# Up projection of a gated feed-forward: the gate's and the value's matmuls issued in turn, each into its own PSUM bank

## The chip, the cores and the metric

The kernel runs on one core of a Trainium2 chip. Its engines work side by side, each through its own list of instructions: TensorE (PE in the profile, its weight loads PEld), VectorE (DVE), ScalarE (ACT), GpSimd (POOL), and SyncE (SP), which issues the DMAs here. They wait for each other by semaphores. The metric is the device time of one execution in microseconds; a run's time is compared with that of the kernel before on the same chip.

## The reference

A linear attention with decay runs over 768 tokens, for 4 sequences and 8 heads of 48 channels. Its output is the input of a gated feed-forward with 1536 hidden units:

```python
for t in range(S):
    kt, vt, rt = (k[:, :, t], v[:, :, t], r[:, :, t])
    cur = np.einsum('bhd,bhe->bhde', u[None] * kt, vt)
    y[:, :, t] = np.einsum('bhd,bhde->bhe', rt, state + cur)
    state = w[None, :, :, None] * state + np.einsum('bhd,bhe->bhde', kt, vt)
...
gate = 1.0 / (1.0 + np.exp(-(x @ w_gate)))
val = x @ w_val
return (gate * val @ w_out).astype(np.float32)
```

`x` is the attention's output as 3072 tokens of 384 channels; `w_gate` and `w_val` are 384 x 1536, `w_out` is 1536 x 384.

## The kernel before

**Tiles and blocks.** The 768 positions go in 12 chunks of 64, which makes 256 columns to a chunk with the four sequences. Two chunks are a tile of 512 columns, so there are six tiles. The 1536 hidden units go in 12 blocks of 128. A *burst* is the attention of one pair of heads of one chunk, 48 in all. A *block* of a tile is one up projection, its gating, and one down projection. The first tile's first four blocks run for each chunk alone, at half the width; this makes 76 blocks: 8 of 256 columns and 68 of 512.

**One block.** Operands are split in a high and a low part (`whi`, `wlo` of the weights, index 0 and 1 of the second axis of `x` and `h`), and a product is three matmuls: low by high, high by high, high by low (`PASS`). The up projection (`Moe.up`, its matmul is L333) sums over 3 x 128 channels, so the gate takes nine matmuls into one PSUM bank and the value nine into another. `Moe.gate` then runs a sigmoid of the gate's bank on ACT (L345), a product with the value's bank on DVE (L346), a copy that makes `h`'s high part on ACT (L347), and a subtraction that makes its low part on POOL (L348). `Moe.down` (L358) adds nine matmuls to three banks `acc` that stay open for the whole tile. Its order changes the output bank at each matmul; in a tile's last block the nine are sorted by output bank instead.

**Banks.** Five PSUM banks are shared under the name `ring` by the gate and the value of each block, by a burst's two score tiles (L245, L246, L255, L256) and by its result `y` (L283, L286). A bank can be written again when its last reader is done: for the gate that is the sigmoid, for the value the product on DVE.

**Order.** The program is a list of 81 steps; a step holds a burst, a block, or both. PE and SP keep the order in which the program issues their instructions (`manual_schedule`), while ACT, DVE and POOL are ordered by a planner that simulates the program when it is built. From step 9 on, a step issues on PE: the up projection of its block, the scores and outer products of its burst, the application of the burst before, and the down projection of the *previous* step's block. In earlier steps up comes behind the burst. Weights arrive as float64 words and are decoded on ACT, DVE and POOL (L175 to L191) in the steps of the first tile; attention is spread over the steps up to the second last tile, and the last tile's steps have none. `store` (L370 to L372) copies a finished tile's three banks and sends them off.

Of the kernel before, what the change touches and what calls it, by code (L numbers as in the profile page):

```python
# [10 lines left out]
F32 = mybir.dt.float32  # L11
# [8 lines left out]
DM, DF = H * D, 1536  # L20
P = 128
# [2 lines left out]
NP = H // 2  # L24
NF = DF // P
CT = B * C
# The program goes in steps of a burst of attention (a pair of heads of a chunk) and a block
# of the feed-forward. Bursts before the first block; blocks whose two chunks go separately;
# blocks of a later tile with a burst beside them; steps in which a burst goes first; the
# steps in which the weights of a block are loaded, and decoded.  # L30
PRE, HALF = NP + 1, 4
SPREAD = [1, 1, 1, 0, 1, 1, 1, 0, 1, 1, 0, 0]
EARLY = 9
LOADW = (-1, 1, 3, 4, 7, 9, 10, 11, 12, 13, 14, 15)
DECW = (1, 4, 5, 6, 9, 10, 11, 12, 13, 14, 15, 16)
# bursts that have more of their work on GpSimd, and on the vector engine
U_POOL, R_DVE = range(3), range(4)
TILES = [[c, c + 1] for c in range(0, NC, 2)]

# [2 lines left out]
def rwkv_then_moe(ctx: ExitStack, tc: tile.TileContext, wd, un, rk, vn, wt, out):  # L42
    nc = tc.nc
# [12 lines left out]
    xp = main.enter_context(tc.tile_pool(name="xp", bufs=2))  # L56
    xsp = main.enter_context(tc.tile_pool(name="xsp", bufs=1))

    # the tensor engine and the loads go in the order of the program
    order = ExitStack()  # L60
    order.enter_context(tc.manual_schedule(engines={mybir.EngineType.PE, mybir.EngineType.SP}))

# [1 line left out]
    wu = const.tile([P, 2, NP], F32, name="wu")  # L64
    nc.sync.dma_start(out=wu, in_=wd)
    w = wu[:, 0]

    # Of a pair of heads: by channel r | k, by token r | k.
    inp = {}
    vz = [const.tile([P, NP, 2, B, 64], F32, name=f"vz{i}") for i in range(2)]  # L70

# [29 lines left out]
    table = const.tile([P, 1], F32, name="table")  # L101
    nc.scalar.activation(table, ident[:, 0:1], AF.Sigmoid)

    # w^0 .. w^96, of each channel; a decay outside 1/2 .. 2, where the powers of a chunk
    # hold, raises the flag instead
    pw = const.tile([P, NP, 97], F32, name="pw")
    nc.vector.memset(pw[:, :, 0], 1.0)
    nc.vector.tensor_scalar(pw[:, :, 1], w, 0.5, 2.0, ALU.max, ALU.min)
# [9 lines left out]
    power(4, 4, 4)  # L118
    power(8, 8, 8)
    power(16, 16, 16)  # L120
    # w^(31 - j); the reverse is w^(i - 32)
    tabk = const.tile([P, NP, C], F32, name="tabk")
    nc.vector.tensor_copy(tabk[:, :, 0:32], pw[:, :, 31::-1])

# [4 lines left out]
    flag = const.tile([1, 1], I32, name="flag")  # L129

    def token_table():
        # w^(95 - j) with the tokens j on the partitions
        power(32, 32, 32)
        power(64, 32, 64)
        tnat_in = hp.tile([P, 512], F32, name="sg").rearrange("q (p a j) -> q p a j", p=NP, a=2)
        for p in range(NP):
            nc.vector.tensor_copy(
                tnat_in[:, p], pw[:, p, 95:31:-1].unsqueeze(1).broadcast_to([P, 2, C])
            )
        tps = ps.tile([P, NP, P], F32, name="ring")  # L140
        for p in range(NP):
            nc.tensor.transpose(
                out=tps[:, p], in_=tnat_in[:, p].rearrange("q a j -> q (a j)"), identity=ident
            )
        nc.scalar.copy(out=tabn[0:64], in_=tps[0:64, :, 64:112])
        nc.scalar.copy(out=tabn[64:128], in_=tps[64:128, :, 0:48])
# [9 lines left out]
        nc.vector.tensor_reduce(total, count[0:1, 0:NP], axis=mybir.AxisListType.X, op=ALU.add)  # L156
        nc.vector.tensor_scalar(flag, total, float(P * NP), None, ALU.is_lt)

# [1 line left out]
    # They come as the words of float64: the high one holds sign, exponent and 20 bits  # L160
    # of the mantissa. Read as float32 and scaled by 2^-112 its exponent is rebiased;
    # three places to the left it is float32's, and the low word's top bits follow.
    # Two slots to a block: first its words, a half to a slot, then the parts hi and lo.
    W3, WH = 3 * DM, 3 * DM // 2
    raw, w32, whi, wlo = {}, {}, {}, {}

# [23 lines left out]
            nc.scalar.copy(out=whi[f][:, c], in_=g)  # L190
            nc.gpsimd.tensor_tensor(wlo[f][:, c], g, whi[f][:, c], ALU.subtract)  # L191

# [1 line left out]
    xt, xs, T, q, sc, yp = {}, {}, {}, {}, {}, {}  # L194

    def bc_b(ap):
# [91 lines left out]
    def to_x(n):  # L288
        c, p = bursts[n]
        ti = next(i for i, cc in enumerate(TILES) if c in cc)  # L290
        if ti not in xt:
            xt[ti] = xp.tile([P, 3, 2, 512], F32R, name="xt")
            xs[ti] = xsp.tile([P, 2, 512], F32R, name="xs")
        x = xt[ti]
        co = CT * TILES[ti].index(c)
        cols = slice(co, co + CT)
        dst = xs[ti][:, :, cols] if p == 3 else x[:, p, :, cols]
        y = yp.pop(n)
        # the last pair of a chunk that is waited for leaves the rows of pair 3 alone
        alone = ti == 0 and p == ORDER[-1]  # L300
        for lo, hi in ((0, 48), (64, 112)) if alone else ((0, 112),):
            nc.scalar.copy(out=dst[lo:hi, 0], in_=y[lo:hi, 0:CT])
            nc.vector.tensor_tensor(dst[lo:hi, 1], y[lo:hi, 0:CT], dst[lo:hi, 0], ALU.subtract)

        def fill(j, cols):
            for lo, to in ((0, 48), (64, 112)):
                nc.sync.dma_start(
                    out=x[to : to + 16, j, :, cols].bitcast(F32),
                    in_=xs[ti][lo + 16 * j : lo + 16 * j + 16, :, cols].bitcast(F32),
                )  # L310

        if ti == 0 and not alone:
            fill(ORDER[-1] if p == 3 else p, cols)
        elif ti and p < 3 and c == TILES[ti][-1]:
            fill(p, slice(0, CT * len(TILES[ti])))

# [1 line left out]
    PASS = ((1, 0), (0, 0), (0, 1))  # L318

    class Moe:  # L320
# [2 lines left out]
            self.pair, self.h = {}, {}  # L323

        def up(self, f):
            self.pair[f] = []
            w = whi[f], wlo[f]
            for g in range(2):
                o = ps.tile([P, 512], F32, name="ring")
                k = 0  # L330
                for kt in range(3):
                    for a, b in PASS:
                        nc.tensor.matmul(  # L333
                            o[:, self.cols], w[a][:, g * DM + kt * P : g * DM + (kt + 1) * P],
                            self.x[:, kt, b, self.cols], start=(k == 0), stop=(k == 8),
                        )
                        k += 1
                self.pair[f].append(o)

        def gate(self, f):  # L340
            a, b = self.pair.pop(f)
# [6 lines left out]
            nc.gpsimd.tensor_tensor(h[:, 1, c], sg[:, c], h[:, 0, c], ALU.subtract)  # L348

        def down(self, f):  # L350
            # the banks' first write clears them whole, so the second half only adds
            h, w = self.h.pop(f), (whi[f], wlo[f])
            todo = [(k, d) for k in range(3) for d in range(3)]
            if f == NF - 1:
                todo.sort(key=lambda kd: kd[1])
            for k, d in todo:
                a, b = PASS[k]
                nc.tensor.matmul(  # L358
                    self.acc[d][:, self.cols], w[a][:, 2 * DM + d * P : 2 * DM + (d + 1) * P],
                    h[:, b, self.cols], start=(f == 0 and k == 0 and self.cols.start == 0),  # L360
                    stop=(f == NF - 1 and k == 2),
                )
# [10 lines left out]
                out=out[d * P : (d + 1) * P, dst], in_=o.rearrange("q (c t) -> q c t", t=CT)  # L373
            )

# [1 line left out]
    halves = [(0, g) for g in range(HALF)] + [(1, g) for g in range(HALF)] + [(2, g) for g in range(HALF, NF)]  # L377
    moe_items = [(0, h, f) for h, f in halves]
    for ti in range(1, len(TILES)):
        moe_items += [(ti, 2, f) for f in range(NF)]  # L380
    # bursts of tile t + 1 in the first steps of tile t
    nb0 = NP * len(TILES[0])
    plan = [(n, None) for n in range(PRE)]
    nxt = PRE
# [43 lines left out]
            store(accs[ti], slice(TILES[ti][0], TILES[ti][-1] + 1))  # L428

    for i, (n, it) in enumerate(plan):  # L430
        # loads, some steps ahead
        later = [k for k, _ in plan[i + 1 :] if k is not None]
        while later and nload < min(len(bursts), later[0] + 3):
            load(*bursts[nload])
            nload += 1
        for f in [f for f, at in enumerate(LOADW) if at == i]:
            load_weights(f)
        nn = n + 2 if n is not None and n + 2 < len(bursts) else None
        m = it and moe_of(it)
        early = i < EARLY  # L440
        if it and not early:
            m.up(it[2])
        if nn is not None:
            decayed(nn)
            decayed_by_token(nn)
        if it and not early:
            m.gate(it[2])
        if n is not None:
            scores(n)
            outer(n)  # L450
            post(n)
        if pend_b is not None:
            apply(pend_b)
            to_x(pend_b)
            c, p = bursts[pend_b]
            if p == ORDER[-1] and c + 2 < NC:
                load_v(c + 2)
            if pend_b == 0:
                load_v(1)
        pend_b = n  # L460
        if nn is not None:
            bonus(nn)
        for fj in [(f, j) for f, at in enumerate(DECW) if at == i for j in range(2)]:
            scale_words(*fj)
        if nn is not None:
            diag(nn)
        for fj in [(f, j) for f, at in enumerate(DECW) if at == i for j in range(2)]:
            join_words(*fj)
            if fj[1] == 1:
                split_weights(fj[0])  # L470
        if it and early:
            m.up(it[2])
            m.gate(it[2])
        if pend_m:
            finish(pend_m)
        pend_m = it
        if i == 24:
            range_flag()
    finish(pend_m)

# [1 line left out]
    order.close()  # L482
    main.close()
    bad = nc.values_load(flag[0:1, 0:1], min_val=0, max_val=1)
# [147 lines left out]
```

## Time and profile before

| What | Value |
|---|---|
| median of 3 runs | 620.98 us |
| lowest and highest run | 620.76 us, 622.1 us |
| profiled execution, first to last instruction (its span) | 618.9 us |
| median less span: what lies around it | 2.1 us |
| busy PE / PEld | 568.8 us / 460.1 us |
| busy DVE / ACT / POOL | 280.8 us / 242.5 us / 294.4 us |
| up projection's matmuls (L333) | 1368 |
| down projection's matmuls (L358) | 684 |

For the profiled execution the span is given, not a time of its own as for the runs, so the runs' median stands beside it. In the profile a row of the timeline has the start in microseconds from the span's beginning, the duration, the engine, the source line, the operation, the tiles written and read, the shape, and how many were merged ("x2"); in brackets is the engine's idle time ahead of it and what ended it. A matmul's duration is longer than the distance to the next matmul's start, since matmuls are pipelined and their ends are modelled: distances of starts are the measure of pace. The table of stretches gives, for a piece of time, the busy time of each engine, the number of its instructions, and the TensorE clock that was granted (1.00 is full).

### The profile page before, as it was taken

Reading aid. Unit: us, or ns where it says so; the run is one execution under the profiler, and the core shown is the slowest. Engines: PE = TensorE matmul, PEld = TensorE weight load, DVE = VectorE, ACT = ScalarE, POOL = GpSimd, SP = SyncE. Lnnn points to the kernel's source line nnn. Section 1 sums busy time; section 2 is a strip of 40 time slices with the busy share of each in tenths; the row PEclk is TensorE's granted clock in tenths of the full one; section 3 lists DMA queues with packets and bytes.
Section 4 is the critical chain, followed back from the end, with each engine's and each line's share of the span. In section 5 each row is a group of like instructions: output and inputs, shape, how many; then the busy total and the mean of one; then the engine's idle time right before and its main releaser. Section 6 shows DMA issues by size and latency. Waiting matters only on the chain. (4 is left out here: it accounts for less than half of the span.)

```text
span 618.9 us, 10939 instructions
## 1 busy us (share of the span) xinstructions
PE 568.8 (92%) x4298; PEld 460.1 (74%) x4298; DVE 280.8 (45%) x568; ACT 242.5 (39%) x656; POOL 294.4 (48%) x298
## 2 busy tenths in 40 slices
PE   1757789887999999999999999999999999999995
PEld 1657678665887877887887787878777777888883
DVE  8889989997043334253334144334253322101011
ACT  2737676654234334145334136334144311211111
POOL 7588999987345335245335237335333311212121
PEclk9868999999999999999999999999999999999998
DMA  7395677233031212331311331311331100010001
GB/s 235 124 295 162 199 252 241 86 115 72 1 112 31 68 41 64 72 111 31 81 43 49 73 112 31 94 39 40 72 112 30 31 10 10 22 38 1 0 1 56
DMA packets 21369, 50.42 MB, mean 81 GB/s; under 512 B 2656, under 2 KB 9312, under 8 KB 21312
## 3 DMA queue, kind: packets, MB, share of 16 engines
q1 hardware_dynamic: 21312, 49.66, 27.2%
q8 instruction: 36, 0.59, 0.4%
q14 instruction: 21, 0.17, 0.1%
HBM read 42.57 MB, written 4.72 MB: 76 GB/s over the span
## 5 line engine op out<-in xcount | busy, mean ns | idle before, releaser
L333 PE MATMUL ring<-xt,whi 128*128 128x512 f32 (+1 forms) x912 | 277.2, 387 | 0.0
L333 PEld LDWEIGHTS ring<-xt,whi 128*128 128x128 f32 x912 | 171.0, 192 | 36.6
L348 POOL TENSOR_TENSOR h<-sg,h 128x512 fp32r<-128x512 f32 (+1 forms) x76 | 98.4, 1294 | 201.8 <-ACT h L347 201.3
L333 PE MATMUL ring<-xt,wlo 128*128 128x512 f32 (+1 forms) x456 | 177.4, 389 | 7.2 <-POOL wlo L191 4.4
L346 DVE TENSOR_TENSOR sg<-ring,sg 128x512 f32<-128x512 f32 (+1 forms) x76 | 50.2, 661 | 216.2 <-PE ring L333 207.6
L234 ACT ACTIVATE T<-ident,q 64x64 f32<-64x64 f32 x384 | 102.1, 335 | 60.3 <-DVE q L229 58.8
L358 PE MATMUL acc<-h,whi 128*128 128x512 f32 (+1 forms) x456 | 115.3, 381 | 8.0 <-POOL h L348 7.6
L333 PEld LDWEIGHTS ring<-xt,wlo 128*128 128x128 f32 x456 | 87.4, 192 | 26.7 <-POOL wlo L191 4.9
L212 POOL TENSOR_TENSOR T<-inp,tabk 64x256 f32<-64x256 f32 x92 | 80.9, 879 | 53.0 <-DMA inp<-in_rk 30.1
L358 PEld LDWEIGHTS acc<-h,whi 128*128 128x128 f32 x456 | 83.0, 188 | 27.1 <-POOL h L348 9.4
L345 ACT ACTIVATE sg<-ring 128x512 f32<-128x512 f32 (+1 forms) x76 | 43.4, 571 | 128.6 <-PE ring L333 127.0
L347 ACT CAST h<-sg 128x512 fp32r<-128x512 f32 (+1 forms) x76 | 45.3, 596 | 109.6 <-DVE sg L346 109.5
L358 PE MATMUL acc<-h,wlo 128*128 128x512 f32 (+1 forms) x228 | 69.9, 406 | 0.2 <-ACT h L347 0.2
L215 POOL TENSOR_TENSOR inp<-inp 128x192 f32<-128x192 f32 x48 | 36.2, 756 | 49.9 <-DMA inp<-in_rk 48.3
L209 DVE TENSOR_TENSOR inp<-inp,tabk 128x256 f32<-128x256 f32 x48 | 27.9, 582 | 60.8 <-DMA inp<-in_rk 60.6
L262 DVE COPY_PREDICATED T<-causal,ring 64x256 f32<-64x256 int32 x96 | 43.0, 447 | 4.9 <-PE ring L256 2.2
L358 PEld LDWEIGHTS acc<-h,wlo 128*128 128x128 f32 x228 | 38.1, 188 | 9.4 <-ACT h L347 0.8
L191 POOL TENSOR_TENSOR wlo<-wf,whi 128x576 fp32r<-128x576 f32 x24 | 41.1, 1726 | 6.6 <-ACT T L234 5.0
L245 PEld LDWEIGHTS ring<-T,inp 48*64 48x64 f32 x384 | 28.0, 141 | 15.8 <-issue 12.2
L228 DVE TENSOR_TENSOR inp<-inp,uns 128x192 f32<-128x192 f32 x45 | 26.1, 580 | 28.9 <-POOL inp L215 28.9
L283 PE MATMUL ring<-T,vz 128*64 128x64 f32 x384 | 34.4, 236 | 3.2 <-ACT T L234 2.1
L246 PE MATMUL ring<-T,inp 48*64 48x64 f32 x384 | 34.3, 233 | 3.2 <-DVE vz L273 1.5
(54 smaller groups left out, 500.9 us busy)
## 6 DMA issues: line engine op xcount, KB each, us to landing
inp<-in_rk SPq DMA_DIRECT2D x48, 448.0 KB, 3.9
wr<-in_wt SPq DMA_DIRECT2D x24, 576.0 KB, 6.9
vz<-in_vn SPq DMA_DIRECT2D x24, 256.0 KB, 4.5
out_y<-o SPq DMA_DIRECT2D x18, 256.0 KB, 2.4
xt<-xs SPq DMA_DIRECT2D x30, 64.0 KB, 2.3
xt<-xs SPq DMA_DIRECT2D x12, 32.0 KB, 2.3
uns<-in_un SPq DMA_DIRECT2D x1, 96.0 KB, 5.4
wu<-in_wd SPq DMA_DIRECT2D x1, 4.0 KB, 1.6
```

The source lines that it names most:

```text
L191: nc.gpsimd.tensor_tensor(wlo[f][:, c], g, whi[f][:, c], ALU.subtract)
L212: eng.tensor_tensor(T[n][lo : lo + 64, k], t[lo : lo + 64, 0], bc_b(tabk[lo : lo + 64, p, ::-1]), ALU.mult)
L215: nc.gpsimd.tensor_tensor(u[:, 0], u[:, 0], u[:, 1], ALU.mult)
L234: nc.scalar.activation(T[n][lo : lo + 64, k, b], ident[lo : lo + 64, lo : lo + 64], AF.Copy, scale=q[n][lo : lo + 64, b : b + 1],)
L262: nc.vector.copy_predicated(T[n][lo : lo + 64, k], bc_b(cmask[lo : lo + 64, lo : lo + 64]), s[lo : lo + 64, 0:256].rearrange("q (b i) -> q ...
L283: nc.tensor.matmul(y[0:64, cs], z[:, 0, b], T[n][:, 0, b], start=True, stop=True)
L333: nc.tensor.matmul(o[:, self.cols], w[a][:, g * DM + kt * P : g * DM + (kt + 1) * P], self.x[:, kt, b, self.cols], start=(k == 0), stop=(k ...
L345: nc.scalar.activation(sg[:, c], a[:, c], AF.Sigmoid)
L346: nc.vector.tensor_tensor(sg[:, c], b[:, c], sg[:, c], ALU.mult)
L347: nc.scalar.copy(out=h[:, 0, c], in_=sg[:, c])
L348: nc.gpsimd.tensor_tensor(h[:, 1, c], sg[:, c], h[:, 0, c], ALU.subtract)
L358: nc.tensor.matmul(self.acc[d][:, self.cols], w[a][:, 2 * DM + d * P : 2 * DM + (d + 1) * P], h[:, b, self.cols], start=(f == 0 and k == 0 ...
```

## The change

The loop over the gate and the value goes inside the loop over the nine products: both banks are taken at the start, and the gate's product *k* is followed by the value's product *k*.

```diff
         def up(self, f):
-            self.pair[f] = []
             w = whi[f], wlo[f]
-            for g in range(2):
-                o = ps.tile([P, 512], F32, name="ring")
-                k = 0
-                for kt in range(3):
-                    for a, b in PASS:
-                        nc.tensor.matmul(
-                            o[:, self.cols], w[a][:, g * DM + kt * P : g * DM + (kt + 1) * P],
-                            self.x[:, kt, b, self.cols], start=(k == 0), stop=(k == 8),
-                        )
-                        k += 1
-                self.pair[f].append(o)
+            o = self.pair[f] = [ps.tile([P, 512], F32, name="ring") for _ in range(2)]
+            for k in range(9):
+                kt, (a, b) = k // 3, PASS[k % 3]
+                for g in range(2):
+                    nc.tensor.matmul(
+                        o[g][:, self.cols], w[a][:, g * DM + kt * P : g * DM + (kt + 1) * P],
+                        self.x[:, kt, b, self.cols], start=(k == 0), stop=(k == 8),
+                    )
```

Each product has the operands it had, and each bank gets its nine products in the same order. The weight that two neighbouring matmuls of one bank share (high by high and high by low) is no longer used twice in a row; the moving operand now is. The rest of the diff takes comments away.

## The prediction
> **What bounds the kernel now.** I read the page first, then the busy time by stretches, then the waits of PE, then the timeline at the places where the two banks of an up projection are filled and emptied. The page's head, its busy shares and its row of granted clock by fortieths:
>
> ```profile
> span 618.9 us, 10939 instructions
> PE 568.8 (92%) x4298; PEld 460.1 (74%) x4298; DVE 280.8 (45%) x568; ACT 242.5 (39%) x656; POOL 294.4 (48%) x298
> ...
> PEclk9868999999999999999999999999999999999998
> ```
>
> The shares are a mean over two very different stages, as the stretches show (length, then busy time of PE, PEld, DVE, ACT, POOL, then clock):
>
> ```profile
> 44.00:134.00 90.00, 74.98 (x804) 64.65 (x802) 85.88 (x150) 59.38 (x169) 84.71 (x75) 0.96 0.58 184
> 134.00:161.00 27.00, 23.32 (x94) 17.78 (x92) 16.66 (x23) 14.16 (x33) 19.13 (x14) 0.94 0.21 47
> 161.00:607.00 446.00, 446.00 (x3114) 357.18 (x3113) 138.82 (x313) 147.30 (x392) 159.41 (x169) 1.00 0.18 49
> ```
>
> From 44 to 134 us DVE is busy 85.88 of 90 and POOL 84.71: attention and the decoding of weights set the pace, and PE has holes. From 161 to 607 us PE is busy all the time at full clock. So in the first stage a delay of PE can vanish in a later hole; in the second every nanosecond of PE counts. The holes, from PE's waits (total, times, longest):
>
> ```profile
> PE acc L358 <- POOL h L348: 7.6, 5, 2.4
> PE ring L333 <- POOL wlo L191: 4.4, 3, 2.3
> PE ring L333 <- DVE sg L346: 2.9, 2, 2.7
> ```
>
> **The change, part by part.** No instruction is added or removed: 18 weight loads and 18 matmuls per block before and after, the same ACT, DVE and POOL work, the same DMAs. Three things move: the pace of the stream, the moment the gate's bank is full, and the moment the value's bank must be free.
>
> *Pace.* Two blocks of the steady end, starts of the matmuls (an entry "x3" is three in a row). First an up (565.47 is the gate's first, 567.57 the value's first), the down behind it and the next up; then the down of a tile's last block, which is sorted by output so that three matmuls in a row go to one bank:
>
> ```profile
> 565.47 0.40 PE L333 MATMUL ring<-xt,wlo 128*128 128x512 f32 x1
> ...
> 567.57 0.39 PE L333 MATMUL ring<-xt,wlo 128*128 128x512 f32 x1
> ...
> 569.66 0.86 PE L358 MATMUL acc<-h,wlo 128*128 128x512 f32 x3
> 570.36 1.52 PE L358 MATMUL acc<-h,whi 128*128 128x512 f32 x6
> 571.72 0.40 PE L333 MATMUL ring<-xt,wlo 128*128 128x512 f32 x1
> ```
> ```profile
> 539.13 0.39 PE L358 MATMUL acc<-h,wlo 128*128 128x512 f32 x1
> ...
> 540.49 0.40 PE L333 MATMUL ring<-xt,wlo 128*128 128x512 f32 x1
> ```
>
> The up takes 569.66 - 565.47 = 4.19 us, 232.8 ns a matmul; the last six of a down take 571.72 - 570.36 = 1.36 us, 226.7 ns. One could think that nine writes to one bank are slow and that the down is quick because it changes bank at every matmul. The sorted down speaks against it: its last six, in two runs of three to one bank and with the moving operand in the up's order, take 540.49 - 539.13 = 1.36 us too. And the up's halves take 2.10 and 2.09 us: the change of bank between them shows nothing. So I take the pace as unchanged, 0 us. The bound on the gain is the down's pace for all full-width up matmuls, whose counts are in the lines by form:
>
> ```profile
> L333 PE MATMUL ring<-xt,whi 128*128 128x512 f32 x816 | 257.3, 396 | 0.0
> L333 PE MATMUL ring<-xt,wlo 128*128 128x512 f32 x408 | 161.9, 397 | 2.9 <-DVE sg L346 2.9
> ```
>
> (816 + 408) x 6.1 ns = 7.5 us. On the other side I know no row of a slower alternation; the same 7.5 us is taken as its bound, by symmetry, an estimate.
>
> *The gate's bank is full later.* Its ninth matmul becomes the block's 17th, so the sigmoid no longer runs beside the value's matmuls. At the very end this is not hidden, because there only one down (2.06 us) stands between the last up and the down that needs its result:
>
> ```profile
> 604.58 0.63 PE L333 MATMUL ring<-xt,whi 128*128 128x512 f32 x2
> 605.31 0.60 ACT L345 ACTIVATE sg<-ring 128x512 f32<-128x512 f32 x1 [2.79 <-PE ring L333]
> ...
> 606.68 0.63 PE L333 MATMUL ring<-xt,whi 128*128 128x512 f32 x2
> 607.41 0.69 DVE L346 TENSOR_TENSOR sg<-ring,sg 128x512 f32<-128x512 f32 x1 [5.55 <-PE ring L333]
> 608.14 0.62 ACT L347 CAST h<-sg 128x512 fp32r<-128x512 f32 x1 [2.23 <-DVE sg L346]
> 608.84 1.28 POOL L348 TENSOR_TENSOR h<-sg,h 128x512 fp32r<-128x512 f32 x1 [4.95 <-ACT h L347]
> 610.17 0.50 PE L358 MATMUL acc<-h,whi 128*128 128x512 f32 x1 [0.36 <-POOLq L485]
> ```
>
> The sigmoid starts 0.10 us after the end of the gate's last matmul (605.21), the multiply 0.10 us after that of the value's (607.31). With the gate's last one matmul ahead of the value's, it ends at 607.31 - 0.23 = 607.08; sigmoid 607.18 to 607.78; a hop of 0.04 (608.10 to 608.14 in the row of the cast); multiply at 607.82 instead of 607.41. PE waits there already (to 610.17, for POOL's part at 610.12), so the whole shift lands on the end: **+0.41 us**. In the other blocks of the PE-bound stage another up of 4.19 us stands between, and the chain from 607.41 to 610.12 takes 2.7 us: it stays hidden, with over 3 us to spare.
>
> *The value's bank must be free earlier,* at the second matmul instead of the tenth: 8 x 0.2328 = 1.86 us. Where the tenth waited already, the wait starts sooner and ends at the same moment, and 17 matmuls follow it instead of 9. The rows: two blocks of the first tile, with the multiply that frees the bank of the second, and one place in the PE-bound stage where the sigmoid that frees a bank runs late:
>
> ```profile
> 106.88 0.64 PE L333 MATMUL ring<-xt,whi 128*128 128x512 f32 x2
> ...
> 109.05 0.50 PE L333 MATMUL ring<-xt,wlo 128*128 128x512 f32 x1 [0.16 <-DVE sg L346]
> ```
> ```profile
> 126.07 0.62 PE L333 MATMUL ring<-xt,whi 128*128 128x512 f32 x2
> ...
> 130.82 0.50 PE L333 MATMUL ring<-xt,wlo 128*128 128x512 f32 x1 [2.73 <-DVE sg L346]
> ```
> ```profile
> 130.09 0.68 DVE L346 TENSOR_TENSOR sg<-ring,sg 128x512 f32<-128x512 f32 x1
> ```
> ```profile
> 359.37 0.57 ACT L345 ACTIVATE sg<-ring 128x512 f32<-128x512 f32 x1
> ...
> 359.43 0.62 PE L333 MATMUL ring<-xt,whi 128*128 128x512 f32 x2
> ```
>
> At 359.43 the value's first matmul would stand; all other banks hold unread tiles, and the sigmoid ends at 359.94; with the hop of 0.05 (130.77 to 130.82) PE waits 359.99 - 359.43 = **+0.56 us**, uncovered. Everywhere else after 161 us a bank is free in time or nearly.
>
> In the first stage the two blocks end 1.86 us later each. The first falls into DVE's backlog. For the second, these are the waits that follow, the sigmoids of that block and the next, and the stretches of 3.41 us on which the granted clock changes:
>
> ```profile
> 143.65 0.50 PE L358 MATMUL acc<-h,whi 128*128 128x512 f32 x1 [1.08 <-POOL h L348]
> ```
> ```profile
> 152.56 0.97 PE L358 MATMUL acc<-h,whi 128*128 128x512 f32 x3 [2.37 <-POOL h L348]
> ```
> ```profile
> 137.62 0.58 ACT L345 ACTIVATE sg<-ring 128x512 f32<-128x512 f32 x1
> ```
> ```profile
> 142.41 0.59 ACT L345 ACTIVATE sg<-ring 128x512 f32<-128x512 f32 x1
> ```
> ```profile
> 126.39:129.80 3.41, 1.70 (x8) 1.04 (x6) 3.38 (x4) 1.59 (x3) 3.33 (x3) 1.00 0.58 223
> ...
> 150.28:153.69 3.41, 1.13 (x5) 0.95 (x6) 2.34 (x3) 1.50 (x5) 3.33 (x4) 1.00 0.00 0
> 153.69:157.11 3.42, 3.42 (x10) 2.65 (x9) 0.01 (x1) 2.08 (x8) 3.42 (x4) 0.50 0.00 0
> ```
>
> After a stretch with PE busy 1.13 of 3.41 us the clock is halved for the next one, costing about 3.42 / 2 = 1.7 us; after one with 1.70 it is not. With the change PE stands from about 126.5 to 130.82, so the stretch from 126.39 is nearly empty, and the matmuls from 130.82 to 133.21 run at half clock: 1.2 us more, a shift of 1.86 + 1.2 = 3.06 us. The waits that follow hold 1.08 + 2.37 = 3.45 us, and what ends them is ACT's and POOL's backlog: the sigmoid at 137.62 runs 4.4 us after its block's matmuls, so it is not made late. All is swallowed by 152.56, and the stretch before 153.69 is now filled, so the half clock there goes: between 0 and -1.7 us. The middle, **-0.85 us**, since the grid of stretches is not tied to the program. Two waits for POOL's wlo in half-width blocks start five matmuls sooner; they lie before 75 us, ahead of the same holes, and I take nothing.
>
> The Trainium skill, in "TensorE: Matmul & The Clock Gate", Part 1, has the same gate: a free-running window of about 3.4 us, half clock after an idle one. The trace agrees with the period (150.28, 153.69, 157.11), and shows it for a window that was a third busy, too.
>
> **Sum**, against the profiled execution: 0 + 0.41 + 0.56 - 0.85 = +0.12 us, span 619.0. The median of the runs, 620.98, is 2.1 us above that span, as what lies around it; so **621.1 us**.
>
> **The rivals.**
> 1. *The alternation is quicker.* Up goes at the down's 226.7 ns: -7.5 us, 620.98 + 0.97 - 7.5 = 614.5. For it: the two paces. Against: the sorted down and the seamless change of bank within the up. A part of it would give 617 to 619. Chance 0.12.
> 2. *The half clock goes for nothing and no bank is late,* because the planner, which orders ACT, DVE and POOL anew, frees banks sooner: 620.98 + 0.41 - 1.7 = 619.7. Chance 0.08.
> 3. *The swallowing fails* (slower). The next block's up begins here:
>
> ```profile
> 136.34 0.39 PE L333 MATMUL ring<-xt,wlo 128*128 128x512 f32 x1
> ```
>
> The place is the wait that ends at 152.56. Its releaser hangs on the sigmoid at 142.41, whose block starts at 136.34 and would end, shifted by 3.06 us, at about 143.6: later than ACT takes it now. If this, or a new order on ACT or POOL, moves POOL's part for that block by more than its slack of about 2 us, the delay stays in front of the PE-bound stage: 620.98 + 0.97 + 1.86 = 623.8, with the half clock 625.0; I take 624.4. For it: the sigmoid that becomes ready so late. Against: ACT and POOL are behind anyway. Chance 0.33.
> 4. *Cycling through banks throttles PE.* If PE paused between alternate banks so that the clock halved, the 1224 matmuls x 0.2328 = 285 us could take up to twice that, 285 us more. The down already changes bank at each matmul, at a clock of 1.00 from 161 to 607 us, so chance 0.02. The Trainium skill names this in the same page, "A second HAM failure mode: psum-queue depth-cycling"; the trace does not agree for the down.
>
> That the order isn't what the diff says is excluded: PE keeps the program's order.
>
> **How the numbers follow.** The forecast has 0.45, the rivals 0.12, 0.08, 0.33 and 0.02. About 0.2% (1.2 us) is what a measurement of this kernel can tell from no change. Rivals 1 and 2 are faster: 0.2; the forecast is within: 0.45; 3 and 4 are slower: 0.35. The range runs from a pace gained by half, 617, to rival 3 with half clock, 625.2; the full pace gain and the throttling are left out, some 0.15 with their fringes.
>
> **What would show it.** Starts of up matmuls 4.19 us apart per block (pace); sigmoid 0.1 us after the 17th matmul, multiply at once behind; PE's wait for POOL in the last down 0.4 us longer; a wait at the second matmul of an up near 359 us, of 0.56; a wait of over 4 us near 126; PE's start on the stage from 153 us no later than before. A pace off by 1 ns is worth 1.2 us and would make the prediction wrong; so would a new order on ACT, DVE or POOL that keeps PE waiting before 161 us.

## The result: slower by 1.5%

| | median | runs | ratio to before |
|---|---|---|---|
| before | 620.87 us (619.7 to 622.1) | 4 | 1 |
| after | 630.52 us (628.9 to 631.85) | 4 | 1.0154 [1.0131, 1.0178] |

The page of the changed kernel's profile, its head and its row of granted clock:

```profile
span 626.7 us, 10963 instructions
PE 577.9 (92%) x4298; PEld 468.0 (75%) x4298; DVE 280.9 (45%) x568; ACT 242.8 (39%) x656; POOL 295.6 (47%) x298
...
PEclk9997898889999999999999999999999999999998
```

Here the up's matmul is L331, the sigmoid L341, the product on DVE L342, the cast L343, the subtraction on POOL L344, the down L354. The span is 7.8 us longer; this execution is the fastest of its four runs, so the median lies further up. The table of stretches, with the columns as in the prediction:

```profile
44.00:134.00 90.00, 72.84 (x707) 64.07 (x707) 82.58 (x143) 58.70 (x167) 80.77 (x69) 0.85 0.50 163
134.00:161.00 27.00, 26.19 (x163) 20.27 (x162) 19.12 (x25) 11.67 (x25) 19.53 (x17) 1.00 0.37 108
161.00:619.00 458.00, 456.41 (x3155) 364.43 (x3154) 141.54 (x319) 151.60 (x405) 164.01 (x173) 1.00 0.17 48
```

The stage from 161 us is almost as full as it was (456.41 of 458 us; before, 446.00 of 446), at clock 1.00. Most of the loss is in the first stage: in the same 90 us PE has issued 707 matmuls instead of 804, DVE has done 143 instructions instead of 150 and POOL 69 instead of 75. The second tile's first up shows how much is lost by its start, in the timelines of before and after:

```profile
167.42 0.40 PE L333 MATMUL ring<-xt,wlo 128*128 128x512 f32 x1
```
```profile
173.39 0.62 PE L331 MATMUL ring<-xt,wlo 128*128 128x512 f32 x2
```

5.97 of the 7.8 us are there already. The waits of PE in the changed kernel:

```profile
PE ring L331 <- DVE sg L342: 7.3, 4, 3.7
PE ring L331 <- POOL wlo L191: 4.3, 3, 2.3
PE ring L331 <- DVE vz L273: 3.5, 2, 2.5
PE acc L354 <- POOL h L344: 1.9, 2, 1.0
```

The wait for POOL's `h` shrank from 7.6 to 1.9 us, and an up now waits for DVE instead: for the product (7.3 against 2.9), and for the attention's update of `vz`, which frees a score bank. But the sum of PE's waits didn't grow. The stretch from 44 us to the second tile's first up, before and after:

```profile
44.00:167.42 123.42, 104.72 (x921) 87.64 (x920) 103.23 (x173) 74.76 (x204) 105.30 (x90) 0.96 0.47 145
```
```profile
44.00:173.39 129.39, 111.42 (x920) 94.08 (x920) 104.39 (x172) 75.43 (x204) 104.10 (x88) 0.89 0.43 136
```

The work in it is the same to within two instructions of each engine. PE stands for 17.97 us instead of 18.70, and is busy for 6.70 us more, at a mean clock of 0.89 instead of 0.96. DVE stands for 25.0 us instead of 20.2, and POOL for 25.3 instead of 18.1. So the stretch is longer because of the slower clock, or because the other engines stand more; the section on the halved clock parts the two.

One place where an up waits for DVE, in PE's and in DVE's timeline:

```profile
107.09 0.39 PE L331 MATMUL ring<-xt,wlo 128*128 128x512 f32 x1
109.99 0.74 PE L331 MATMUL ring<-xt,wlo 128*128 128x512 f32 x1 [2.51 <-DVE vz L273]
```
```profile
105.60 1.56 DVE L228 TENSOR_TENSOR inp<-inp,uns 128x192 f32<-128x192 f32 x1 [0.49 <-POOL inp L215]
107.09 1.96 DVE L183 SCALAR_TENSOR_TENSOR wf<-wr,wf 128x576 int32<-128x576 int32 x1
...
109.43 0.41 DVE L273 SCALAR_TENSOR_TENSOR vz<-vz,pw,ring 48x192 f32<-48x192 f32 x1
...
110.54 0.34 DVE L229 TENSOR_REDUCE q<-inp 128x4 f32<-128x192 f32 x1
110.80 0.41 DVE L342 TENSOR_TENSOR sg<-ring,sg 128x256 f32<-128x256 f32 x1
```

The gate's first matmul runs at 107.09, the value's first 2.9 us later, when the update of `vz` at 109.43 is done. Meanwhile DVE works through decoding (L183) and the attention's L262 to L229, and the product of the block before comes behind them all. At this place PE waits for the attention, not for the product. In the kernel before that product runs ahead of all this:

```profile
97.22 1.03 DVE L209 TENSOR_TENSOR inp<-inp,tabk 128x256 f32<-128x256 f32 x1
98.17 0.41 DVE L346 TENSOR_TENSOR sg<-ring,sg 128x256 f32<-128x256 f32 x1
```

So DVE's list of instructions is no longer the same. PE keeps the program's order, but the planner orders ACT, DVE and POOL from its own simulation of the program, and the change moved that. The number of DVE's other instructions ahead of the product of the first tile's blocks 2 to 13, from the two programs:

```
block     2    3    4    5    6    7    8    9   10   11   12   13
before  102  117  130  136  151  159  168  182  197  211  223  231
after   105  118  133  138  153  163  180  189  204  216  231  233
```

The product stands later in every one, in the 8th block by twelve instructions (the place above). In all, 144 of DVE's 568 places hold another instruction than before, 148 of ACT's and 108 of POOL's. Two theories follow. **A:** the new order of ACT, DVE and POOL costs the time. **B:** PE's own order does, by the early bank or the late gate.

### The profile page after: what moved, and what is told of

Its sections match the earlier page's. It is cut to its first block, busy times and chain, and to the rows that moved or that the text cites. A ratio compares the mean times of both kernels' runs of the same rounds, so it can differ in the third digit from the quotient of the medians.

```text
span 626.7 us, 10963 instructions
## 1 busy us (share of the span) xinstructions
PE 577.9 (92%) x4298; PEld 468.0 (75%) x4298; DVE 280.9 (45%) x568; ACT 242.8 (39%) x656; POOL 295.6 (47%) x298
## 5 line engine op out<-in xcount | busy, mean ns | idle before, releaser
L331 PE MATMUL ring<-xt,whi 128*128 128x512 f32 (+1 forms) x912 | 245.8, 393 | 0.0
L331 PEld LDWEIGHTS ring<-xt,whi 128*128 128x128 f32 x912 | 172.9, 197 | 36.9
L344 POOL TENSOR_TENSOR h<-sg,h 128x512 fp32r<-128x512 f32 (+1 forms) x76 | 101.3, 1332 | 183.6 <-ACT h L343 182.0
L331 PE MATMUL ring<-xt,wlo 128*128 128x512 f32 (+1 forms) x456 | 145.0, 396 | 15.2 <-DVE sg L342 7.3
L342 DVE TENSOR_TENSOR sg<-ring,sg 128x512 f32<-128x512 f32 (+1 forms) x76 | 50.2, 661 | 204.8 <-ACT sg L341 199.1
L341 ACT ACTIVATE sg<-ring 128x512 f32<-128x512 f32 (+1 forms) x76 | 43.5, 573 | 230.5 <-PE ring L331 230.5
L212 POOL TENSOR_TENSOR T<-inp,tabk 64x256 f32<-64x256 f32 x92 | 79.5, 864 | 81.3 <-PE ring L286 45.0
L354 PE MATMUL acc<-h,whi 128*128 128x512 f32 (+1 forms) x456 | 115.0, 383 | 2.6 <-POOL h L344 1.9
L331 PEld LDWEIGHTS ring<-xt,wlo 128*128 128x128 f32 x456 | 87.7, 196 | 36.4 <-DVE sg L342 9.1
L354 PEld LDWEIGHTS acc<-h,whi 128*128 128x128 f32 x456 | 83.8, 191 | 20.7 <-POOL h L344 2.7
L354 PE MATMUL acc<-h,wlo 128*128 128x512 f32 (+1 forms) x228 | 70.8, 410 | 0.4 <-ACT h L343 0.4
L343 ACT CAST h<-sg 128x512 fp32r<-128x512 f32 (+1 forms) x76 | 45.3, 596 | 59.6 <-DVE sg L342 59.5
L209 DVE TENSOR_TENSOR inp<-inp,tabk 128x256 f32<-128x256 f32 x48 | 26.3, 547 | 89.2 <-DMA inp<-in_rk 89.1
L354 PEld LDWEIGHTS acc<-h,wlo 128*128 128x128 f32 x228 | 38.8, 191 | 10.0 <-ACT h L343 1.5
L262 DVE COPY_PREDICATED T<-causal,ring 64x256 f32<-64x256 int32 x96 | 43.0, 447 | 3.5 <-PE ring L256 0.5
```

The lines of the kernel that those rows point to most:

```text
L212: eng.tensor_tensor(T[n][lo : lo + 64, k], t[lo : lo + 64, 0], bc_b(tabk[lo : lo + 64, p, ::-1]), ALU.mult)
L262: nc.vector.copy_predicated(T[n][lo : lo + 64, k], bc_b(cmask[lo : lo + 64, lo : lo + 64]), s[lo : lo + 64, 0:256].rearrange("q (b i) -> q ...
L331: nc.tensor.matmul(o[g][:, self.cols], w[a][:, g * DM + kt * P : g * DM + (kt + 1) * P], self.x[:, kt, b, self.cols], start=(k == 0), stop ...
L341: nc.scalar.activation(sg[:, c], a[:, c], AF.Sigmoid)
L342: nc.vector.tensor_tensor(sg[:, c], b[:, c], sg[:, c], ALU.mult)
L343: nc.scalar.copy(out=h[:, 0, c], in_=sg[:, c])
```

## Experiments

Unless said otherwise a kernel is compared over three rounds with the kernel before on the same chip. An order is held by edges without a semaphore, put at the end of the program: they only tell the planner which instruction of an engine comes behind which. In the traces of the first two runs below the three engines run exactly the order that was to be held. Line numbers in these kernels differ; the tiles tell which instruction a row is. The diffs are shortened to what matters, with loops and conditions written in short.

### One half of the change at a time

```diff
     finish(pend_m)
+    for engine, places in ISSUE.items():
+        mine = [k for k in nc.cur_bb.bb.instructions if k.engine == engine and type(k).__name__ in COMPUTE]
+        for a, b in zip(places, places[1:]):
+            tc.add_manual_dep(mine[b], mine[a].name, NoSync, reason="issue order")
```

**The change on PE, the order of before elsewhere:**

> The change on PE as it is, but ACT, DVE and POOL issue their instructions in exactly the order that they had before the change (their order is pinned). Theory A (the planner's new order of ACT, DVE and POOL costs the time): about 621 to 622 us, the prediction's own sum, with +0.4 at the end and +0.6 near 359 us. Theory B (PE's order itself costs it: the value's bank is wanted sooner, the gate's is full later): about 630 us as with the change, whatever the order on the other engines.

Measured: 621.28 us, 1.0006 [0.9991, 1.0022].

**Nine and nine on PE, the changed kernel's order elsewhere:**

> The mirror image: PE issues nine gate matmuls and then nine value matmuls as before, but ACT, DVE and POOL are pinned to the order that they have with the change. Theory A: about 629 to 630 us. Theory B: about 621 us. If both share the cost, x1 and x2 lie in between and their excesses over before add up to about 9.7 us, or to less where they meet in the same holes.

Measured: 626.77 us, 1.0106 [1.0074, 1.0138].

Theory A holds in the main: PE's order alone costs nothing that can be measured. The other engines' order alone costs 1.1%, less than the 629 to 630 us that the theory asked for, and both together cost 1.5%. The two intervals just overlap (up to 1.0138, from 1.0131), so a part of the loss may need both.

Two more kernels take one part of PE's new order each, with before's order elsewhere:

```diff
-            for g, k in [(g, k) for g in range(2) for k in range(9)]:
+            for g, k in [(0, 0), (1, 0)] + [(0, k) for k in range(1, 9)] + [(1, k) for k in range(1, 9)]:   # early bank
+            for g, k in [(0, k) for k in range(8)] + [(1, k) for k in range(8)] + [(0, 8), (1, 8)]:         # late gate
```

**Early bank:**

> One part alone, with the other engines pinned to their order before: gate 0, value 0, then the gate's other eight and the value's other eight. The value's bank is wanted at the second matmul as with the change, but the gate's is full at the 10th matmul instead of the 17th. Theory B with the bank as its cause: as far above before as x1. Theory B with the late gate as its cause, or theory A: within 1 us of before (here I expect +0.6 near 359 us, nothing at the end).

Measured: 620.21 us, 0.9984 [0.9969, 0.9998]. Once more with five rounds:

> The kernel of the third run once more, with more rounds. If the early bank has a gain of its own: 0.9970 to 0.9995 again. If that was scatter: 0.9995 to 1.0015.

Measured: 620.16 us, 0.9993 [0.9975, 1.0010]. The value lies in the band for a gain of its own (0.9970 to 0.9995), but its interval takes in 1: a small gain is neither shown nor excluded.

**Late gate:**

> The other part alone, again with the other engines pinned to their order before: eight gate matmuls, eight value matmuls, then the last of each. The gate's bank is full at the 17th matmul, the value's bank is wanted at the 9th instead of the 10th. Theory B with the late gate as its cause: as far above before as x1. With the bank as its cause, or theory A: +0.4 us, the piece at the end of the kernel.

Measured: 621.86 us, 1.0017 [1.0002, 1.0032]. Its last up and the last down's wait:

```profile
604.99 0.40 PE L405 MATMUL ring<-xt,wlo 128*128 128x512 f32 x1
...
612.59 0.50 PE L428 MATMUL acc<-h,whi 128*128 128x512 f32 x1 [0.62 <-POOLq L569]
```

From one to the other it is 7.60 us. In the kernel before it is 7.22 (602.95, the first row of the fence below, to 610.17), and in the early-bank kernel 7.22 too. The late gate costs 0.38 us at the end, and the early bank nothing there.

### Which tile

```diff
+            turns = [(k, g) for k in range(9) for g in range(2)]
+            if self.ti == 0:            # in the mirror: self.ti > 0
+                turns.sort(key=lambda t: t[1])
+            for k, g in turns:
```

The planner is free in both. **In turn from the second tile on:**

> Nine and nine in the blocks of the first tile, in turn from the second tile on, planner free (its order in the first tile stays that of before). All of the loss in the first tile's order: 621.0 to 621.8 (the last block's 0.4 us and up to 0.6 us for a bank). Rival, a loss of pace or banks in the 60 later blocks: 624 or more.

Measured: 623.46 us, 1.0043 [1.0027, 1.0060], between the two theories. **In turn in the first tile alone:**

> In turn in the blocks of the first tile, nine and nine from the second tile on, planner free (it takes the new order of the changed kernel in the first tile). All of the loss in the first tile: 628.5 to 630.5. Rival, a loss in the later blocks: 624 to 626.

Measured: 626.67 us, 1.0101 [1.0077, 1.0125], less than expected. So about two thirds of the loss are made in the first tile, and there is a second one behind it, of 2.6 us where I had priced 0.41 and 0.56. In the changed kernel's trace 1.8 of the 7.8 us come behind the second tile's first up: 0.38 at the end, and most of the rest at one place, here on PE and on DVE:

```profile
373.58 0.40 PE L331 MATMUL ring<-xt,wlo 128*128 128x512 f32 x1
374.95 0.50 PE L331 MATMUL ring<-xt,wlo 128*128 128x512 f32 x1 [0.97 <-DVE sg L342]
```
```profile
373.87 0.42 DVE L209 TENSOR_TENSOR inp<-inp,tabk 128x256 f32<-128x256 f32 x1 [5.32 <-DMA inp<-in_rk]
374.21 0.69 DVE L342 TENSOR_TENSOR sg<-ring,sg 128x512 f32<-128x512 f32 x1
```

Here the product stands one place later, behind L209, and L209 waits for a load: DVE is idle for 5.32 us with the product behind it, and the up is 1.14 us late (374.95 - 373.58 = 1.37, less the pace of 0.23). In the kernel before, the same two instructions in the other order:

```profile
363.66 0.69 DVE L346 TENSOR_TENSOR sg<-ring,sg 128x512 f32<-128x512 f32 x1 [0.44 <-PE ring L333]
369.03 0.43 DVE L209 TENSOR_TENSOR inp<-inp,tabk 128x256 f32<-128x256 f32 x1 [4.68 <-DMA inp<-in_rk]
```

The load is late there too, and no product waits behind it. The run with turns from the second tile on has PE's wait at the same block (0.58 us, at 369.64).

### Which part of the new order

First with the planner free but for one edge per product on DVE:

```diff
+    for a, b in (each product of the first and later tiles, and its neighbour on DVE):
+        tc.add_manual_dep(mine[b], mine[a].name, NoSync, reason="issue order")
```

**Nine and nine, products held late:**

> Order as before on PE (nine and nine); every product on DVE is only held behind the DVE instruction that stands ahead of it in the changed kernel's program, and the planner orders all else as it likes. Theory, the late product on DVE alone (it keeps the value's bank and so PE): 625 to 628, near the 626.8 of the run with the whole new order. Rival, the rest of the new order (decoding and attention work on ACT and POOL): 621 to 622.

Measured: 629.69 us, 1.0153 [1.0129, 1.0177]: more than the whole new order gave under nine and nine. **The change, products held early:**

> The change on PE; every product on DVE is only held ahead of the DVE instruction that follows it in the program before, and the planner orders all else as it likes. Theory, the late product: 621 to 623, with no wait of PE at 107 us and about 4 us of it near 127. Rival, the rest of the new order: 628 to 630, as the changed kernel.

Measured: 622.38 us, 1.0027 [1.0005, 1.0048]: most of the loss is gone. Both times agree with the late product as the cause. PE's waits in the second run do not: there is no wait of 4 us near 127, and in all PE waits for the product as long as in the changed kernel (7.3 us):

```profile
PE ring L337 <- DVE sg L348: 7.4, 4, 2.9
```

Besides, the planner arranged the rest around the edges again (in the first of them, 118 places on DVE, 105 on ACT and 60 on POOL differ from before), so they don't isolate it. The next ones hold every place.

**One product later** (the change, before's order, the 8th block's product moved 8 places):

> The change on PE, the order of before on ACT, DVE and POOL, but for one instruction: DVE's product of the first tile's 8th block stands 8 places later (the changed kernel has it 12 later). If late products are the cause: a wait of PE of 2 to 4 us at the next up's second matmul (about 101 us), and 622.5 to 625 where the run without this had 621.3. Rival, one late product is swallowed like the two late uppings that were predicted: 621 to 621.8.

Measured: 621.7 us, 1.0015 [0.9992, 1.0037]. PE doesn't wait at the next up, but two and four blocks later:

```profile
110.53 0.50 PE L406 MATMUL ring<-xt,wlo 128*128 128x512 f32 x1 [1.85 <-DVE sg L417]
...
131.73 0.63 PE L406 MATMUL ring<-xt,wlo 128*128 128x512 f32 x1 [2.78 <-DVE sg L417]
```

They are no longer than without the move (5.7 us in two waits there, 4.6 here), and the time is the same: one late product is swallowed. **All products late,** nothing else moved, under nine and nine:

> Nine and nine, before's order on ACT, DVE and POOL, but DVE's products stand where the changed kernel has them (up to 8 places later; in three blocks 1 to 4 places short of it). Product's place is the cause: 624 to 627. Rival, the rest of the order: 620.5 to 621.5.

Measured: 628.34 us, 1.0109 [1.0089, 1.0129]. Under the change:

> The same order under the change on PE. Product's place: 627 to 630.5. Rival, the rest: 621 to 622.

Measured: 633.56 us, 1.0209 [1.0175, 1.0244]. Late products alone cost as much as the whole new order, or more; both times lie above the theory's range. **The mirror,** the changed kernel's order with the products alone put back:

> The change on PE with its own order on ACT, DVE and POOL, but DVE's products stand where before has them (in the 8th and the 10th to 13th block only part of the way). Product's place: 621 to 624. Rival, the rest: 628 to 630.5.

Measured: 630.67 us, 1.0159 [1.0135, 1.0182]. This is what the theory of the product's place forbids. Its DVE waits from 44 to 161 us say why:

```profile
DVE sg L417 <- ACT sg L416: 12.8, 9, 2.9
```

DVE takes the product up earlier and stands there for the sigmoid, which ACT still has late. So the next two move all four instructions of the gating (sigmoid, product, cast, subtraction). **Put back in the changed kernel's order:**

> The change on PE; decoding and attention in the changed kernel's order on ACT, DVE and POOL, but all four instructions of the gating where before has them (one product only part of the way). The gating carries the loss: 620.5 to 623.5. Rival, the new order of decoding and attention costs by itself: 627 to 631.

Measured: 636.15 us, 1.0237 [1.0199, 1.0275], the slowest of all, and above both ranges. **Put late in before's order:**

> The change on PE; decoding and attention in the order of before, all four instructions of the gating where the changed kernel has them (in three blocks 1 or 2 places short of it). The gating carries the loss: 628 to 632. Rival: 621 to 623.

Measured: 630.86 us, 1.0152 [1.0116, 1.0188].

| order under the change on PE | gating as before | gating late |
|---|---|---|
| decoding and attention as before | 1.0006 | 1.0152 |
| decoding and attention new | 1.0237 | 1.0154 (the change) |

So the place of one kind of instruction doesn't decide it. Late gating is enough for the whole loss where the rest stands as before. But with the new order of the rest, early gating is worse still, and then PE waits for the last of the gating, in one wait of its timeline for 6 us:

```profile
165.72 1.65 PE L429 MATMUL acc<-h,whi 128*128 128x512 f32 x3 [6.04 <-POOL h L419]
```

I read this as a matter of how the lists of three engines fit each other; what makes one set fit was not found. One count parts all these kernels, POOL's instructions from 44 to 134 us, here of the changed kernel with the early products and with the late gating:

```profile
44.00:134.00 90.00, 73.89 (x772) 63.48 (x771) 84.39 (x144) 58.58 (x168) 81.64 (x74) 0.92 0.56 181
```
```profile
44.00:134.00 90.00, 71.90 (x724) 63.28 (x723) 74.53 (x140) 55.92 (x162) 73.76 (x69) 0.87 0.53 170
```

Every kernel at 1.0057 or below has done 74 or 75 there, every kernel at 1.01 or above 68 to 71. DVE's count overlaps (143 to 150 against 138 to 146). The count marks how far the work has come; it is no cause.

### Products earlier than before

If late is bad, is earlier good? Five products of the first tile are put where their operands are there in the profile of before, first under nine and nine:

> Nine and nine as before, the order of before on all engines, but for five of DVE's products in the first tile (blocks 7, 9, 10, 11, 13), which stand 5, 2, 3, 4 and 1 places earlier, at the first place where their operands are there in the profile of before. If the product's place sets PE's waits: the 2.7 us wait near 131 us goes and the time is 617 to 619.5. Rival, what it is put ahead of (decoding, attention) is late instead: 620.5 to 622.

Measured: 622.91 us, 1.0031 [1.0011, 1.0051]. Under the change:

> The change on PE, the order of before, with the same five products earlier. If the product's place sets PE's waits: the 4.2 us wait near 128 us shrinks to under 2, and 617.5 to 620. Rival, as above: 621 to 622.5.

Measured: 624.26 us, 1.0057 [1.0040, 1.0073]. The rival was the nearer one, and both times lie above its range. In the first of the two the 2.7 us wait near 131 us is gone, and what was overtaken is late instead: PE now stands 3.9 us in one wait for `vz`. No version was found whose gain over the kernel before held when it was measured again.

### The halved clock

The changed kernel with its own order held, PE kept working at three of its waits:

```diff
+                    AGAIN = {(256, 2): 28, (0, 4): 11, (0, 6): 11}    # first tile only
+                    for _ in range(AGAIN.get((self.cols.start, f), 0) if k == g == 0 else 0):
+                        nc.tensor.matmul(o[g][:, self.cols], ..., start=True, stop=True)
```

> The changed kernel with its own order held on ACT, DVE and POOL; in three blocks of the first tile (7th, 9th and 11th, where PE stands 3.7, 2.5 and 2.7 us for a bank) the gate's first product is computed 28, 11 and 11 times more into its own bank, so that PE works while it waits; the result is the same. If the halved clock behind these waits is part of the loss: no half clock near 93 to 100, 110 to 113 and 130 to 134 us, and 626.5 to 628.5. If only the waiting counts, because DVE and POOL set the pace there: 629.5 to 631.5, with the half clock gone.

Measured: 628.36 us, 1.0121 [1.0083, 1.0158]. The stretch and the clock:

```profile
44.00:134.00 90.00, 76.12 (x812) 66.38 (x810) 84.65 (x145) 59.60 (x168) 82.93 (x71) 0.96 0.52 169
```
```profile
PEclk9999799999999999999999999999999999999999
```

At these three waits the half clock went: the stretch has 0.96 instead of 0.85, as much as the kernel before. Most of the loss stayed, and the second tile's first up still comes 4.83 us later than before, where it was 5.97:

```profile
172.25 0.62 PE L413 MATMUL ring<-xt,wlo 128*128 128x512 f32 x2
```

So the clock is not the main cause. The time lies at the upper edge of the range for a part played by the clock, and the 2.2 us between the medians fit one, but the intervals overlap; its size stays open.

## Why the prediction was wrong

**Pace: right.** Two blocks of the steady end of the changed kernel:

```profile
560.28 0.62 PE L331 MATMUL ring<-xt,wlo 128*128 128x512 f32 x2
...
564.48 0.86 PE L354 MATMUL acc<-h,wlo 128*128 128x512 f32 x3
...
566.53 0.62 PE L331 MATMUL ring<-xt,wlo 128*128 128x512 f32 x2
```

4.20 us for the up and 2.05 for the down, as before. Rivals 1 and 4 (quicker, throttled) fall with it: the clock is 1.00 from 161 us on.

**The end: right.** Predicted +0.41 us. From the last up's first matmul to the one that waits, before and after:

```profile
602.95 0.40 PE L333 MATMUL ring<-xt,wlo 128*128 128x512 f32 x1
```
```profile
610.26 0.62 PE L331 MATMUL ring<-xt,wlo 128*128 128x512 f32 x2
...
617.86 0.50 PE L354 MATMUL acc<-h,whi 128*128 128x512 f32 x1 [0.62 <-POOLq L481]
```

617.86 - 610.26 is 7.60 against 7.22: +0.38.

**A wait of 0.56 us near 359 us: wrong,** it isn't there. With before's order held, ACT and PE at that place:

```profile
358.77 0.57 ACT L416 ACTIVATE sg<-ring 128x512 f32<-128x512 f32 x1
```
```profile
359.41 0.62 PE L406 MATMUL ring<-xt,wlo 128*128 128x512 f32 x2
```

The sigmoid is 0.60 us earlier than before (359.37) and PE 0.22 later (359.19), 0.82 between them; a shift of 0.56 is enough to take the wait away. I had treated the distance between the two engines as fixed. What moved it was not looked into.

**The first stage: here it failed.** The step was "All is swallowed by 152.56", worked out from the waits and backlogs of the kernel before. With before's order held it is what happens. The forecast wait of over 4 us near 126 us is there, and the second tile begins 0.22 us later than before:

```profile
132.47 0.79 PE L406 MATMUL ring<-xt,wlo 128*128 128x512 f32 x1 [4.16 <-DVE sg L417]
...
167.64 0.62 PE L406 MATMUL ring<-xt,wlo 128*128 128x512 f32 x2
```

The size was too hopeful (+0.22 for -0.85), and the sum with it is well within 0.2%: 621.28 measured, 621.1 forecast. That it is so near is in part luck, as the missing +0.56 makes up for half of this error. But the changed kernel doesn't run that order. I knew that a planner orders ACT, DVE and POOL, wrote that a new order "would make the prediction wrong", and still moved only PE's instructions in the sum. So the step that failed is the -0.85 us: it took the other engines' lists as fixed. In its place the runs showed +5.97 us by the second tile's first up, with the new order and PE's together.

**Rival 3** named a new order on ACT or POOL and put 624.4 us and a chance of 0.33 on it. The direction was right, the price was not: it came from slacks of the old order (1.86 us of shift, and the half clock), which say nothing of a new one. Held late, the gating alone cost 10.0 us (630.86 against 620.83 for before on that chip), over five times that shift. **Rival 2** took the planner for a help that frees banks sooner; in the first tile it put the products later.

What made the planner choose this order was not tried. The sigmoid is ready only when the 17th matmul is done, some 1.9 us later than before, so that other work may go ahead of it in the planner's simulation; that is an argument, not a result.

## What to carry to other kernels

Where a planner orders some of the engines, an edit to one engine's order is two changes: the one in the diff, and a new list on every engine that the planner owns. Compare those lists first; and to learn what the edit itself is worth, hold the other engines' order and time it so. Don't mend a bad order by moving one kind of instruction: here either half of a matched order, alone, was as bad as the other order or worse, while one edge per product, with the planner free to fit the rest, got back most of the loss (1.0027 instead of 1.0154). And don't take one engine's waits for the loss: in that last kernel PE waits for the product as long as in the changed one.

## What the runs showed of the hardware

The TensorE clock came back later than I had assumed. In the changed kernel, stretches of 3.41 us on the clock's own grid:

```profile
89.54:92.95 3.41, 1.01 (x8) 0.72 (x6) 3.33 (x4) 2.27 (x7) 3.41 (x4) 1.00 0.91 359
92.95:96.36 3.41, 2.16 (x10) 2.16 (x11) 3.35 (x8) 1.81 (x7) 3.26 (x4) 0.50 0.27 108
96.36:99.78 3.42, 3.42 (x41) 3.14 (x40) 3.04 (x7) 2.04 (x4) 3.15 (x3) 0.50 0.03 7
...
106.61:110.02 3.41, 0.90 (x8) 0.62 (x6) 3.35 (x5) 1.86 (x4) 3.41 (x4) 1.00 0.84 193
110.02:113.43 3.41, 3.41 (x8) 2.73 (x9) 3.41 (x9) 2.85 (x10) 1.32 (x3) 0.50 1.01 358
113.43:116.85 3.42, 3.42 (x45) 2.62 (x44) 2.23 (x5) 1.30 (x3) 3.42 (x3) 1.00 0.24 88
```

After a stretch in which PE was busy for 1.01 or 0.90 of 3.41 us the clock is halved. Where the halved stretch is full, the next one is at full clock again; where it is busy for only 2.16 of 3.41 us, the next one is halved as well. I had counted one stretch, 1.7 us, for each wait. Nor does the busy share alone tell when the clock is halved: a stretch with 2.00 of 3.42 us busy (48.57 to 51.99) was followed by a halved one here, and in the kernel before one with 1.70 was not.
